# Single maxima between the groups of half sums and half differences in the front of a two-branch attention kernel

## The chip, the cores and the metric

The kernel runs on one core of one Trainium2 chip. The metric is the device time of one execution in microseconds (us). A measurement of a kernel is the median over several executions.

## The reference

For one sequence of 2048 positions and a model width of 512 the reference mixes two attention branches by a gate. Branch A is a local dilated attention (32 heads of 16, window of 8 keys with a stride of 2); branch B is a full attention whose 32 query heads share one key head and one value head.

```python
x = A_x
g = _sigmoid((x * gate_w).sum(-1, keepdims=True))
a = _A_ref(x, A_wqkv, A_wo)
b = _B_ref(x, B_wq, B_wk, B_wv, B_wo)
return g * a + (1 - g) * b
...
# branch B
q = (x @ wq).reshape(B, S, H, Dh).transpose(0, 2, 1, 3)
k = x @ wk
v = x @ wv
scores = jnp.einsum("bhqd,bkd->bhqk", q, k) * (Dh ** -0.5)
p = _softmax(scores, axis=-1)
o = jnp.einsum("bhqk,bkd->bhqd", p, v)
return o.transpose(0, 2, 1, 3).reshape(B, S, H * Dh) @ wo
```

The softmax of branch B takes the maximum of 2048 scores for every query and head off before the exponential, and these maxima are what this case is about.

## The kernel before

**The work on branch B.** The 2048 x 32 queries are cut into 32 units of 512 positions and 4 heads (`NU`). Queries lie with head dimensions on the partitions, and two heads share the 128 rows: head parity `odd` uses rows 64 * odd and up, so two matmuls on different row halves run side by side. The loop `for s in range(NS + 1)` (L1131) has 16 steps for each unit, 512 in all. A step computes the scores of 128 keys for two pairs of heads (`exp_pair`, L475, matmuls L480, exponential on ScalarE L482), and adds the weighted values of the step before into `po` (`weighted`, L487, eight row-and-column tiles of L490). The weighted values of a unit need its maxima: they stand in two extra rows of the query tile (rows 62 and 63 of each half), put there by `shift_a` to `shift_d`.

**The maxima.** A maximum here is over 512 keys, for 128 queries of one head; there are 2048 of them (`NF`), 64 for each unit. A slot `(v, pr, t, kc)` names two of them, one for each row half. There are three ways to compute them:

- `fill_pair` (L345): two matmuls into the two banks of `m2` (called `pm` in the profile) and one VectorE reduction over both (L350).
- `fill_one` (L354): one matmul into one bank, `m1` (`ps`) or another, and one VectorE reduction (L361). The second single of a slot waits in the list `half`.
- half sums and half differences: max(a, b) = (a + b)/2 + |a - b|/2. With the half sum and half difference of two blocks of keys in place of the keys (`half_keys`, `half_parts`, kept in `kcd`), `fill_diff` (L417) puts the differences of two slots into `m2`, ScalarE takes their absolute values into `dd` (L425), and later `fill_sum` (L430) puts the sums of one row half into a one-bank tile and a single VectorE instruction (L435) adds, reduces over the keys, and so finishes two maxima. `pend` lists sums still to come. Row half 0 goes into `m1`, row half 1 into `po`. In the front `dd` is one buffer; in the output rows it is two.

**The order.** Everything is issued in an order written out when the program is built. A planner keeps a time for each engine (`clk`), the time each bank comes free (`free`) and the time the absolute values are ready (`ready_d`), with fixed durations (`T_R` 0.23, `T_LAT` 0.20, `T_RED1` 0.61, `T_TTR` 0.66 us and so on), and decides by them what is issued next. Each engine then takes its instructions in that order.

**The front.** `stream` (L720) runs the projections in the front, and later the output rows. The two row halves of a projection are two sequences; where a single or a sum is due, it takes the place of one half's matmul and the other half goes on. In the front `pooled` is True, and `po` can take singles too. The front first projects the queries (lumps `q`, with `queries_post`), then branch A's queries, keys and values (64 lumps `a`, with `a_post`: two copies on ScalarE, L251 and L252, and additions on GpSimd). From the lumps (0, 3) to (0, 6) of branch A on, `half_sel` and `half_keys` make the half keys. From then on `paired` holds whenever two neighbouring slots can be taken together, and only differences and sums are issued, until two lumps before the end. Units are stacked (`stack`) up to the eighth in the front, and `fillable` admits only stacked units.

**The loop.** Each step may do one pair in `m2` and one single in `m1`. The single is issued only while `singles(s)` holds: twice the steps up to unit 31 plus 20 for each output row to come is less than what is left (`to_go`). When eight and four output rows are due (`out_phase`, L759), the stream runs again with `pooled` False and does half sums beside them. The last four rows are spread over the steps after the maxima (`spread`, products L836). If a unit's maxima come late, `pause` fills them in at once.

Of the kernel before, what the change touches and what calls it, by code (L numbers as in the profile page):

```python
# [49 lines left out]
def gated_mix_kernel(ctx, tc, xt, wa, wk, wq, wo_a, wo_b, out):  # L50
# [28 lines left out]
    m1 = pp.tile([P, 512], F32, name="ps")  # L79
    po = pp.tile([P, 512], F32, name="po")  # L80
# [5 lines left out]
    clk = {"pe": 0.0, "act": 0.0, "dve": 0.0}  # L86

    def after(eng, ready, dur):
        clk[eng] = max(clk[eng], ready) + dur
        return clk[eng]  # L90
# [214 lines left out]
    slots = [(v, pr, t, kc) for kc in range(2) for v in range(2) for pr in range(2) for t in range(4)]  # L305
    slots += [(v, pr, t, kc) for v in range(2) for pr in range(2) for t in range(4) for kc in range(2, 4)]
    slots += [(v, pr, t, kc) for v in range(2, NU) for pr in range(2) for t in range(4) for kc in range(4)]
    half = []
    free = {"m2": 0.0, "m1": 0.0, "e0": 0.0, "e1": 0.0, "po": 0.0}
    tasks, shifted, pm = [], set(), []  # L310
    hooks, pool, done = [], 0.0, set()
# [1 line left out]
    def fillable():  # L313
        return bool(half) or bool(slots) and slots[0][0] < len(stacked) and stacked[slots[0][0]] <= clk["pe"]

    def unit_tile(v):
        for x in (v, v + 1):
            if x < NU and x not in left:
                mx[x] = wp.tile([P, 2, 2, 4, 4], F32, name="mx", bufs=3)
                if pe:  # L320
                    nc.gpsimd.memset(mx[x], -FMAX)
                    charge(250)
                else:
                    nc.scalar.activation(mx[x].rearrange("p b i t k -> p (b i t k)"), ident[:, 0:64], AF.Identity, scale=0.0, bias=mk[:, 6:7])
                left[x] = NF // NU
        return mx[v]

    def max_mm(dst, v, pr, t, kc, odd):
        b = 64 * odd
        nc.tensor.matmul(dst, qst[home(v)[0]][b:b + 62, pr, t * P:(t + 1) * P], kst[b:b + 62, kc * 512:(kc + 1) * 512], start=True, stop=True)  # L330

    def to_go():
        return 2 * len(slots) + len(half)

    def filled(v, n):
        left[v] -= n
        if not left[v]:
            ms = wp.tile([P, 2, 2, 8], F32, name="ms")
            m = mx.pop(v).rearrange("p b i t k -> p b (i t) k")
            nc.vector.tensor_reduce(ms, m.unsqueeze(2).to_broadcast([P, 2, 2, 8, 4]), AX.X, ALU.max)  # L340
            mt = wp.tile([P, 32], F32, name="mt")
            nc.vector.transpose(mt, ms.rearrange("p b x y -> p (b x y)"))
            tasks.append((after("dve", 0, 0.66) + (2.0 if kcd and not pe else 0.1), shift_a, (v, mt)))
# [7 lines left out]
        free[key] = after("dve", after("pe", 0, T_R) + T_LAT, T_RED2) + 0.08  # L351
        filled(v, 2)

    def fill_one(dst=m1, key="m1"):  # L354
        if not half:
            v, pr, t, kc = slots.pop(0)
            half.extend([(v, pr, t, kc, 0), (v, pr, t, kc, 1)])
        v, pr, t, kc, odd = half.pop(0)
        m = unit_tile(v)
        max_mm(dst, v, pr, t, kc, odd)  # L360
        nc.vector.tensor_reduce(m[:, odd, pr, t, kc:kc + 1], dst, AX.X, ALU.max)  # L361
        free[key] = after("dve", after("pe", 0, T_R) + T_LAT, T_RED1) + 0.08
        filled(v, 1)


    sel, kcd, dd, pend, ready_d, formed, ended, wants = [], [], [], [], [0.0, 0.0], set(), set(), []
# [43 lines left out]
    def paired():  # L410
        return len(slots) > 1 and slots[0][3] % 2 == 0 and slots[0][3] // 2 in formed and slots[1] == slots[0][:3] + (slots[0][3] + 1,) and fillable()

    def half_mm(dst, v, pr, t, kc, x, odd):
        b = 64 * odd
        nc.tensor.matmul(dst, qst[home(v)[0]][b:b + 62, pr, t * P:(t + 1) * P], kcd[0][b:b + 62, kc // 2, x, :], start=True, stop=True)  # L415

    def fill_diff():  # L417
# [9 lines left out]
        free["m2"] = ready_d[1]  # L427
        pend.extend([(v, pr, t, kc, 0), (v, pr, t, kc, 1)])

    def fill_sum():  # L430
        v, pr, t, kc, odd = pend.pop(0)
        m = unit_tile(v)
        dst, key = ((m1, "m1"), (po, "po"))[odd]
        half_mm(dst, v, pr, t, kc, 0, odd)
        nc.vector.tensor_tensor_reduce(dd[0][:, odd], dst, dd[0][:, odd], 1.0, -FMAX, ALU.add, ALU.max, m[:, odd, pr, t, kc:kc + 1])  # L435
        free[key] = after("dve", max(clk["pe"] + T_R + T_LAT, ready_d[odd]), T_TTR) + 0.08
        filled(v, 2)
# [35 lines left out]
    pe, pexp, exped = [], {}, {}  # L473
# [246 lines left out]
    def stream(seq, mm, done, pooled):  # L720

        at, told = [0, 0], 0
        ended.clear()
        while min(at) < len(seq):
            single, odd = None, -1
            if wants and all(free[k] <= clk["pe"] + 0.1 for k in (("m1", "po") if wants[0] else ("m2",))):
                half_keys(wants.pop(0))
            if pend:
                if free[("m1", "po")[pend[0][4]]] <= clk["pe"] + 0.1 and ready_d[pend[0][4]] <= clk["pe"] + 0.4:
                    single, odd = fill_sum, pend[0][4]  # L730
            elif paired() and not half or 1 in wants:
                pass
            elif fillable() and free["m1"] <= clk["pe"] + 0.1:
                single, odd = lambda: fill_one(m1, "m1"), half[0][4] if half else 0
            elif pooled and fillable() and free["po"] <= clk["pe"] + 0.1:
                single, odd = lambda: fill_one(po, "po"), half[0][4] if half else 0
            dur = 0.0
            for b in (0, 1) if odd != 1 else (1, 0):
                if b == odd:
                    now = clk["pe"]  # L740
                    single()
                    clk["pe"] = now
                elif at[b] < len(seq):
                    dur = mm(b, seq[at[b]])
                    at[b] += 1
            after("pe", 0, dur or T_R)
            if ended or 0 in wants:
                pass
            elif paired():
                if not half and not pend and max(free["m2"], clk["dve"] - 1.2) <= clk["pe"] + 0.1:  # L750
                    fill_diff()
            elif slots and fillable() and free["m2"] <= clk["pe"] + 0.1:
                clk["pe"] = max(clk["pe"], free["m2"])
                fill_pair(m2, "m2")
            while told < min(at):
                told += 1
                done(seq[told - 1])

    def out_phase(js, n, whole_unit):  # L759

        m = 3 * (C + n)
        items = {}

        def mm(b, at):
            x, j, i = at
            if j not in items:
                items[j] = out_items(j, n)
                clk["pe"] = max(clk["pe"], free[f"e{x % 2}"])
            st, mv = items[j][i]
            h = slice(64 * b, 64 * b + 64)  # L770
            nc.tensor.matmul(eb[x % 2][:, b, :], st()[h], mv[h], start=(i == 0), stop=(i == m - 1))  # L771
            return T_R

        def done(at):
            x, j, i = at
            if i % 4 == 3:
                run_tasks()
                run_pool()
            if x == len(js) - 1 and i == m - 5:
                ended.add(1)  # L780
            if x == 0 and i == 1:
                turn(j, 1)
            if x == 0 and i == 6:
                later.pop(j)()
            if i == 3 * n and j != js[-1]:
                prepare(js[x + 1], n)
            if i == m - 5 and j != js[-1]:
                turn(js[x + 1], 1 - x % 2)
            if i == m - 1:
                out_store(j, x % 2)  # L790
                if j != js[-1]:
                    later.pop(js[x + 1])()

        if whole_unit:
            formed.update((0, 1))
            free["po"] = max(free["po"], clk["dve"] + 0.1)
            dd[:] = [px.tile([P, 2, 512], F32, name="pexp", bufs=6) for _ in range(2)]
        stream([(x, j, i) for x, j in enumerate(js) for i in range(m)], mm, done, False)
        while pend:
            odd = pend[0][4]  # L800
            clk["pe"] = max(clk["pe"], free[("m1", "po")[odd]], ready_d[odd] - 0.3)
            fill_sum()
            clk["pe"] += T_R
        settle("sum", 0)
        formed.clear()
# [309 lines left out]

    front = [(eb[1], "e1"), (eb[0], "e0"), (m2, "m2")]
    stream([(x, i) for x in range(len(lumps)) for i in range(3 * C)], mm, done_mm, True)
    assert not pend
    formed.clear()
    for kind in ("add", "store"):  # L1120
        settle(kind, 0)
# [9 lines left out]
    for s in range(NS + 1):  # L1131
# [11 lines left out]
        v = min(x[0][0] for x in (half, slots, [(NU,)]) if x)  # L1143
# [105 lines left out]
```

## Time and profile before

| | |
|---|---|
| median of 3 runs | 1487.6 us (1487.28 to 1487.6) |
| span of the profiled execution | 1485.2 us (2.4 us under the median; the execution's own time is not listed apart) |
| busy: PE, DVE, ACT, POOL | 1472.3, 1195.4, 1276.8, 1029.6 us |
| chain that ended last | PE 91%, ACT 3%, POOL 2% |
| costliest on ACT | exponentials L482, 988.4 us |
| costliest on DVE | pairs L350 623.6 us, singles L361 308.8 us |

The span is the time from the first to the last instruction of one profiled execution. Busy times are of the engine's own instructions; PE counts a matmul to its modelled end, so that a busy PE is not PE at its peak. In rows by instruction the columns are the line, the engine, the operation, what is written and read, and how often; then busy time and mean duration in ns; then the idle time just before, and who ended it. In rows by time the columns are start, duration, engine, line, operation and count, with the idle time before in brackets. PEld is the loading of weights, which runs beside PE.

### The profile page before, as it was taken

How to read it: one execution, taken by the hardware profiler on the slowest of the kernel's cores; microseconds unless marked ns; L12 is line 12 of the kernel's file. 1: busy time of each engine (PE TensorE's matmuls, PEld its weight loads, DVE VectorE, ACT ScalarE, POOL GpSimd, SP SyncE). 2: the span in 40 equal slices, each digit the busy share in tenths (PEclk: the TensorE clock that was granted, in tenths of full speed). 3: DMA queues.
4: the chain of work that ended last, by engine and by line, in shares of the span. 5: the costliest groups of instructions: out<-in, count | busy, mean ns of one | idle time of the engine just before them, and what ended most of it. 6: DMA issues, size and time to landing. Idle time of an engine off the chain costs nothing.

```text
span 1485.2 us, 29515 instructions
## 1 busy us (share of the span) xinstructions
PE 1472.3 (99%) x10996; PEld 707.2 (48%) x10996; DVE 1195.4 (80%) x1824; ACT 1276.8 (86%) x1654; POOL 1029.6 (69%) x1824
## 2 busy tenths in 40 slices
PE   9999999999999999999999999999999999999998
PEld 5999989433333333333333476333333363333343
DVE  6976667788888888888888888888888888888822
ACT  4468988999999999999999988999999978999975
POOL 7876988787888988988888999788797130110121
PEclk9999999999999999999999999999999999999999
DMA  6754233021120111211211202021020010000011
GB/s 222 210 151 135 88 105 107 28 84 52 55 85 18 67 59 41 70 41 41 70 43 40 81 31 89 12 70 51 31 70 12 12 34 19 2 1 1 16 30 43
DMA packets 54136, 89.86 MB, mean 60 GB/s; under 512 B 18849, under 2 KB 35289, under 8 KB 49769
## 3 DMA queue, kind: packets, MB, share of 16 engines
q1 hardware_dynamic: 46856, 48.98, 11.0%
q0 software_dynamic: 6560, 37.95, 7.6%
q8 instruction: 86, 1.41, 0.4%
q10 hardware_dynamic: 576, 1.05, 0.2%
q14 instruction: 58, 0.47, 0.1%
HBM read 60.07 MB, written 27.35 MB: 59 GB/s over the span
## 4 chain that ended last, share of the span: by engine, by line
PE 91%; ACT 3%; POOL 2%; issue 1%; DVE 1%; DMA 0%; DVEq 0%; POOLq 0%; ACTq 0%
PE po L490 34%; PE pe L480 26%; PE pm L330 8%; PE pe L1082 7%; PE ps L330 5%; PE pe L771 4%; PE pm L415 2%; PE ps L415 1%; PE pm L836 1%; PE po L415 1%; ACT dd L425 1%; POOL qlo L222 1%; POOL qraw L215 1%; PE pe L185 1%; ACT qhi L221 0%
## 5 line engine op out<-in xcount | busy, mean ns | idle before, releaser
L482 ACT ACTIVATE pexp<-pe 128x1024 f32<-128x1024 f32 x1022 | 988.4, 1022 | 102.7 <-PE pe L480 99.1
L350 DVE TENSOR_REDUCE mx<-pm 128x2 f32<-128x1024 f32 x511 | 623.6, 1220 | 143.8 <-PE pm L330 140.5
L490 PE MATMUL po<-pexp,vst 128*32 128x512 f32 x4096 | 545.5, 605 | 0.0
L480 PE MATMUL pe<-qst,kst 64*128 64x512 f32 x1916 | 523.6, 454 | 1.6 <-ACT pexp L482 1.0
L480 PEld LDWEIGHTS pe<-qst,kst 64*128 64x128 f32 x1916 | 215.2, 184 | 417.3 <-ACT pexp L482 408.2
L361 DVE TENSOR_REDUCE mx<-ps 128x1 f32<-128x512 f32 x454 | 308.8, 680 | 3.6 <-PE ps L330 3.5
L330 PE MATMUL pm<-kst,qst 62*128 62x512 f32 x971 | 197.7, 399 | 0.7 <-ACT pexp L482 0.4
L550 POOL TENSOR_TENSOR pr<-aext 128x256 f32<-128x256 f32 x256 | 182.1, 738 | 1.5 <-DMA aext<-ad 1.2
L330 PE MATMUL ps<-kst,qst 62*128 62x512 f32 x428 | 179.9, 420 | 0.0
L610 POOL TENSOR_TENSOR oa<-oa,av 128x256 f32<-128x256 f32 x224 | 164.0, 732 | 15.2
L490 PEld LDWEIGHTS po<-pexp,vst 128*32 128x32 f32 x4096 | 80.6, 108 | 176.3 <-issue 167.4
L607 POOL TENSOR_TENSOR av<-aext,lg 128x256 f32<-128x256 f32 x224 | 139.3, 622 | 12.5
L330 PEld LDWEIGHTS ps<-kst,qst 62*128 62x128 f32 x428 | 78.6, 184 | 69.3 <-DVE mx L361 65.9
L1082 PE MATMUL pe<-wal,xh 64*128 64x384 f32 (+1 forms) x504 | 109.9, 337 | 0.0
L1082 PE MATMUL pe<-wah,xh 64*128 64x384 f32 (+1 forms) x504 | 109.4, 338 | 0.4 <-ACT gate L255 0.4
L1082 PE MATMUL pe<-wah,xl 64*128 64x384 f32 (+1 forms) x504 | 109.6, 337 | 0.0
L516 POOL TENSOR_TENSOR rl<-rl,gate_t 128x16 f32<-128x16 f32 x31 | 6.9, 221 | 143.9 <-DVE rl L510 143.9
L425 ACT ACTIVATE dd<-pm 128x512 f32<-128x512 f32 x164 | 90.9, 607 | 17.8 <-PE pm L415 11.9
L435 DVE CUSTOM_DVE_ANT_0 dd<-ps,dd 128x512 f32<-128x512 f32 x82 | 56.7, 692 | 54.6 <-PE ps L415 29.5
L330 PEld LDWEIGHTS pm<-kst,qst 62*128 62x128 f32 x971 | 93.8, 187 | 6.3 <-DVE mx L350 3.2
L556 POOL TENSOR_TENSOR tr<-pr 128x512 f32<-128x512 f32 x64 | 81.7, 1276 | 4.2
L556 POOL TENSOR_TENSOR tr<-tr 128x256 f32<-128x256 f32 (+1 forms) x128 | 72.5, 566 | 7.9
(218 smaller groups left out, 1898.2 us busy)
## 6 DMA issues: line engine op xcount, KB each, us to landing
aext<-ad POOLq DMA_DIRECT2D x32, 1056.0 KB, 5.4
ad<-stage SPq DMA_DIRECT2D x32, 384.0 KB
qst<-qd SPq DMA_DIRECT2D x60, 128.0 KB
xraw<-xt SPq DMA_DIRECT2D x16, 256.0 KB
qd<-qhi SPq DMA_DIRECT2D x16, 256.0 KB
qd<-qlo SPq DMA_DIRECT2D x16, 256.0 KB
qst<-qd SPq DMA_DIRECT2D x60, 64.0 KB
qst<-ml SPq DMA_DIRECT2D x212, 2.0 KB
```

The source lines that it names most:

```text
L330: nc.tensor.matmul(dst, qst[home(v)[0]][b:b + 62, pr, t * P:(t + 1) * P], kst[b:b + 62, kc * 512:(kc + 1) * 512], start=True, stop=True)
L350: nc.vector.tensor_reduce(m[:, :, pr, t, kc], dst, AX.X, ALU.max)
L361: nc.vector.tensor_reduce(m[:, odd, pr, t, kc:kc + 1], dst, AX.X, ALU.max)
L425: nc.scalar.activation(dd[0][:, odd], m2[:, odd, :], AF.Abs)
L480: nc.tensor.matmul(bank[:, odd, :], kst[b:b + 64, kt * P:(kt + 1) * P], qst[home(u)[0]][b:b + 64, pr, :], start=True, stop=True)
L482: nc.scalar.activation(e, bank, AF.Exp, scale=SCALE)
L490: nc.tensor.matmul(po[32 * i:32 * i + 32, :], vst[:, kt, :], pexp[s, i // 2][:, i % 2, :], start=(kt == 0), stop=(kt == NJ - 1))
L550: nc.gpsimd.tensor_mul(pr[:, k], q, e[:, o:o + NH, AC:2 * AC])
L556: nc.gpsimd.tensor_add(nx, cur[:, :, 0:n], cur[:, :, n:2 * n])
L607: nc.gpsimd.tensor_mul(av, e[:, o:o + NH, 2 * AC:].rearrange("p j (h d) -> p j h d", d=DH), lg[:, w].unsqueeze(3).to_broadcast([P, NH, AG, ...
L610: nc.gpsimd.tensor_add(ao, ao, av)
L1082: nc.tensor.matmul(front[2 if x == last else x % 2][0][:, b, :n], l[h], r[h], start=(i == 0), stop=(i == 3 * C - 1))
```

## The change

In the front, once half keys exist, a list `extra` is kept beside `half`. When no sum is pending, or the next pending sum is at least 0.6 us from ready by plan, when VectorE's planned end is at most 0.45 us ahead of PE, and when `m1` or `po` is free, a single maximum is issued from `extra` into whichever of the two comes free first. If `extra` is empty, two neighbouring slots are taken off and become four singles. `fill_sum` also takes whichever of `m1` and `po` comes free first (`bank_free`), no longer one by row half. What is left in `extra` when the front ends goes to the head of `half`. `to_go` counts `extra` too.

```diff
--- before.py
+++ after.py
@@ -305,7 +305,7 @@
     slots = [(v, pr, t, kc) for kc in range(2) for v in range(2) for pr in range(2) for t in range(4)]
     slots += [(v, pr, t, kc) for v in range(2) for pr in range(2) for t in range(4) for kc in range(2, 4)]
     slots += [(v, pr, t, kc) for v in range(2, NU) for pr in range(2) for t in range(4) for kc in range(4)]
-    half = []
+    half, extra = [], []
     free = {"m2": 0.0, "m1": 0.0, "e0": 0.0, "e1": 0.0, "po": 0.0}
     tasks, shifted, pm = [], set(), []
     hooks, pool, done = [], 0.0, set()
@@ -330,7 +330,7 @@
         nc.tensor.matmul(dst, qst[home(v)[0]][b:b + 62, pr, t * P:(t + 1) * P], kst[b:b + 62, kc * 512:(kc + 1) * 512], start=True, stop=True)
 
     def to_go():
-        return 2 * len(slots) + len(half)
+        return 2 * len(slots) + len(half) + len(extra)
 
     def filled(v, n):
         left[v] -= n
@@ -351,11 +351,11 @@
         free[key] = after("dve", after("pe", 0, T_R) + T_LAT, T_RED2) + 0.08
         filled(v, 2)
 
-    def fill_one(dst=m1, key="m1"):
-        if not half:
+    def fill_one(dst=m1, key="m1", queue=None):
+        if not half and not queue:
             v, pr, t, kc = slots.pop(0)
             half.extend([(v, pr, t, kc, 0), (v, pr, t, kc, 1)])
-        v, pr, t, kc, odd = half.pop(0)
+        v, pr, t, kc, odd = (queue or half).pop(0)
         m = unit_tile(v)
         max_mm(dst, v, pr, t, kc, odd)
         nc.vector.tensor_reduce(m[:, odd, pr, t, kc:kc + 1], dst, AX.X, ALU.max)
@@ -427,10 +427,13 @@
         free["m2"] = ready_d[1]
         pend.extend([(v, pr, t, kc, 0), (v, pr, t, kc, 1)])
 
+    def bank_free():
+        return min(((m1, "m1"), (po, "po")), key=lambda x: free[x[1]])
+
     def fill_sum():
         v, pr, t, kc, odd = pend.pop(0)
         m = unit_tile(v)
-        dst, key = ((m1, "m1"), (po, "po"))[odd]
+        dst, key = bank_free()
         half_mm(dst, v, pr, t, kc, 0, odd)
         nc.vector.tensor_tensor_reduce(dd[0][:, odd], dst, dd[0][:, odd], 1.0, -FMAX, ALU.add, ALU.max, m[:, odd, pr, t, kc:kc + 1])
         free[key] = after("dve", max(clk["pe"] + T_R + T_LAT, ready_d[odd]), T_TTR) + 0.08
@@ -725,9 +728,15 @@
             single, odd = None, -1
             if wants and all(free[k] <= clk["pe"] + 0.1 for k in (("m1", "po") if wants[0] else ("m2",))):
                 half_keys(wants.pop(0))
-            if pend:
-                if free[("m1", "po")[pend[0][4]]] <= clk["pe"] + 0.1 and ready_d[pend[0][4]] <= clk["pe"] + 0.4:
-                    single, odd = fill_sum, pend[0][4]
+            bank, key = bank_free()
+            if pend and free[key] <= clk["pe"] + 0.1 and ready_d[pend[0][4]] <= clk["pe"] + 0.4:
+                single, odd = fill_sum, pend[0][4]
+            elif pooled and (extra or paired()) and not half and not wants and free[key] <= clk["pe"] + 0.1 and clk["dve"] <= clk["pe"] + 0.45 and (not pend or ready_d[pend[0][4]] >= clk["pe"] + 0.6):
+                if not extra:
+                    extra.extend(x + (odd,) for x in (slots.pop(0), slots.pop(0)) for odd in range(2))
+                single, odd = lambda: fill_one(bank, key, extra), extra[0][4]
+            elif pend:
+                pass
             elif paired() and not half or 1 in wants:
                 pass
             elif fillable() and free["m1"] <= clk["pe"] + 0.1:
@@ -798,7 +807,7 @@
         stream([(x, j, i) for x, j in enumerate(js) for i in range(m)], mm, done, False)
         while pend:
             odd = pend[0][4]
-            clk["pe"] = max(clk["pe"], free[("m1", "po")[odd]], ready_d[odd] - 0.3)
+            clk["pe"] = max(clk["pe"], free[bank_free()[1]], ready_d[odd] - 0.3)
             fill_sum()
             clk["pe"] += T_R
         settle("sum", 0)
@@ -1116,6 +1125,7 @@
     front = [(eb[1], "e1"), (eb[0], "e0"), (m2, "m2")]
     stream([(x, i) for x in range(len(lumps)) for i in range(3 * C)], mm, done_mm, True)
     assert not pend
+    half[:0] = extra
     formed.clear()
     for kind in ("add", "store"):
         settle(kind, 0)
```

## The prediction

> **What bounds the kernel now.** I read the head of the page first, then the busy time of each engine by stage, then the instructions in order of time in one stretch of each stage, and last the waits of the front.
>
> ```profile
> span 1485.2 us, 29515 instructions
> PE 1472.3 (99%) x10996; PEld 707.2 (48%) x10996; DVE 1195.4 (80%) x1824; ACT 1276.8 (86%) x1654; POOL 1029.6 (69%) x1824
> ...
> 105.00:262.00 157.00, 155.99 (x1576) 142.82 (x1575) 106.76 (x330) 135.76 (x317) 129.71 (x204) 1.00 0.35 109
> ...
> 272.00:848.00 576.00, 575.23 (x4016) 205.59 (x4012) 499.16 (x607) 529.12 (x570) 492.35 (x940) 1.00 0.17 55
> ...
> 1227.00:1410.00 183.00, 183.00 (x1275) 64.30 (x1274) 157.97 (x189) 165.67 (x172) 19.92 (x46) 1.00 0.03 8
> ```
>
> The columns of the last three are PE, PEld, DVE, ACT, POOL, clock. 105 to 262 us is the part of the front in which half sums and half differences run beside the projections of branch A; 272 to 848 and 1227 to 1410 us are the loop over steps. PE is fed in all of them and the clock is full (1.00), so the time is the sum of what PE is given, plus short waits. DVE, which the change loads, has 157.00 - 106.76 = 50.2 us free in the front; ACT has 21.2. What a maximum costs on PE in the loop is read from five steps in a row (the eight weighted products start a step):
>
> ```profile
> 400.11 1.06 PE L490 MATMUL po<-pexp,vst 128*32 128x512 f32 x8
> ...
> 401.67 0.46 PE L330 MATMUL ps<-kst,qst 62*128 62x512 f32 x1
> ...
> 402.29 1.06 PE L490 MATMUL po<-pexp,vst 128*32 128x512 f32 x8
> ...
> 403.63 0.40 PE L330 MATMUL pm<-kst,qst 62*128 62x512 f32 x2
> ...
> 403.86 0.40 PE L480 MATMUL pe<-qst,kst 64*128 64x512 f32 x2
> ...
> 403.92 3.81 ACT L482 ACTIVATE pexp<-pe 128x1024 f32<-128x1024 f32 x4 [0.27 <-PE pe L480]
> ...
> 404.20 1.06 PE L490 MATMUL po<-pexp,vst 128*32 128x512 f32 x8
> ...
> 405.76 0.39 PE L330 MATMUL ps<-kst,qst 62*128 62x512 f32 x1
> ...
> 406.35 1.06 PE L490 MATMUL po<-pexp,vst 128*32 128x512 f32 x8
> ...
> 408.24 1.06 PE L490 MATMUL po<-pexp,vst 128*32 128x512 f32 x8
> ```
>
> Steps with a single maximum (`ps`) last 402.29 - 400.11 = 2.18 and 406.35 - 404.20 = 2.15 us, those without 404.20 - 402.29 = 1.91 and 408.24 - 406.35 = 1.89. A single costs about 0.26 us here; that fits one slot of a row-tiled pair (403.86 - 403.63 = 0.23), because its own row half has four matmuls between two weighted groups where the other has three. I take 0.25. No more can be had by it: four exponentials take 3.81 us, so 1.905 for the two of a step, and a step without a single is already as long as its exponentials.
>
> **What moves.** Nothing is added to the work as a whole: a single given out in the front is one less in the loop, where a single is only issued while more is left than the pairs of the remaining steps and the output rows can take. What is left after the front now is large enough that it is issued nearly to the end:
>
> ```profile
> L361 DVE TENSOR_REDUCE mx<-ps 128x1 f32<-128x512 f32 x454 | 308.8, 680 | 3.6 <-PE ps L330 3.5
> ...
> 0.00:267.00 267.00, 32.27 (x50) 1.00 0.47 143
> ...
> 0.00:267.00 267.00, 32.92 (x27) 1.00 0.47 143
> ...
> 0.00:267.00 267.00, 90.92 (x164) 1.00 0.47 143
> ```
>
> The last three are the front's instructions of L361 (50 singles), of L350 (27 pairs) and of L425 (164 absolute differences, each of which with its sum stands for two maxima): 50 + 54 + 328 = 432 of 2048. Eight units of queries are stacked in the front, 8 x 64 = 512 maxima, so at most 80 more can be done there at all.
>
> **How many singles.** Each needs DVE for 0.68 us (L361's mean); 50.2 us of idle DVE hold at most 50.2 / 0.68 = 74. The condition asks for more than idle time: a bank free, DVE's planned end within 0.45 us, and the next sum at least 0.6 us off (or none pending). The waits of 105 to 262 us say how often that can be:
>
> ```profile
> DVE dd L435 <- PE ps L415: 29.3, 51, 1.2
> DVE dd L435 <- ACT dd L425: 17.1, 22, 1.2
> ACT dd L425 <- PE pm L415: 11.3, 18, 0.9
> PEld pm L415 <- ACT dd L425: 10.6, 37, 0.6
> ...
> ACT dd L425 <- DVE mx L435: 4.5, 8, 0.9
> ...
> L251 ACT ACTIVATE stage<-pe 128x384 f32<-128x384 f32 x53 | 26.1, 492 | 3.9 <-PE pe L1082 2.3 <-POOL wal L84 0.8 <-issue 0.2
> ```
>
> DVE waits 73 times for a sum, (29.3 + 17.1) / 73 = 0.64 us on average and up to 1.2. With the planner's constants, a difference that finds ACT free has its first absolute value ready 0.23 + 0.20 + 0.52 + 0.10 = 1.05 us after its issue, while the sums before it keep DVE booked to 0.9 or 1.0 after it: once the booking is within 0.45, the next sum is no more than 0.6 off, and no single fits. Where a projection block's two copies stand ahead on ACT (0.8 us in the plan), the sum is up to 0.8 later and one fits. There are 53 such blocks in the stretch. Between the half of 73 waits that are above their mean (37) and one for each block (53) I take 45 singles.
>
> **What they cost in the front.** Projection pairs follow each other here:
>
> ```profile
> 160.26 0.35 PE L1082 MATMUL pe<-wah,xl 64*128 64x384 f32 x2
> ...
> 160.43 0.35 PE L1082 MATMUL pe<-wah,xh 64*128 64x384 f32 x2
> ...
> 160.61 0.35 PE L1082 MATMUL pe<-wal,xh 64*128 64x384 f32 x2
> ```
>
> 0.175 us for a pair. 53 blocks x 12 pairs x 0.175 = 111 us; 156 / 2 = 78 differences in the stretch (a count of L425's instructions there, 78/79 by L435) at 0.23 for the pair of differences and 2 x 0.115 for the two sums, 36 us. 111 + 36 = 147, and 10.6 us of PE's weight loads waiting for ACT makes 158 of 157. So the account closes, and a single in the front costs half a slot, 0.23 / 2 = 0.115 us: the stream lets it take one row half while the other goes on with the projection, and evens the halves out. Gain for each: 0.25 - 0.115 = 0.135 us.
>
> To this comes a wait w for each single, which the trace of before does not show. Below: a longer cycle between two differences can swallow part of the 10.6 us that PE waits for ACT, 10.6 / 45 = 0.24 each at the very most. Above: PE runs in order, and if a single pushes the following sum by its whole DVE time, 0.68, and this comes back to PE through ACT, it is 0.68. The condition keeps the single out of the way of the next sum by plan (0.45 + 0.61 of DVE against 0.6 + 0.4 + latency of the sum's matmul), so I take the value near the rows that exist: ACT has waited for DVE's sums 8 times, 4.5 us in all, and if half of the singles bring one such short push of about 0.15, w is near 0.05 net. 45 x (0.135 - 0.05) = 3.8 us.
>
> That sums take whichever bank is free costs nothing by itself: without singles the two banks come free in turn as now. It is what lets a sum start while a single holds the other bank; without it, each single would hold up the sum of one parity. The same choice is made in the output rows' stream, where no singles are given out, and in turn again.
>
> **The end.** Now the maxima come too late for the last unit, and a pause is made for them:
>
> ```profile
> 1411.30 1.07 PE L490 MATMUL po<-pexp,vst 128*32 128x512 f32 x8
> ...
> 1413.43 1.06 PE L490 MATMUL po<-pexp,vst 128*32 128x512 f32 x8
> ...
> 1414.42 0.50 PE L330 MATMUL pe<-kst,qst 62*128 62x512 f32 x1
> ...
> 1416.31 3.83 ACT L482 ACTIVATE pexp<-pe 128x1024 f32<-128x1024 f32 x4 [1.48 <-PE pe L480]
> ...
> 1420.41 1.07 PE L490 MATMUL po<-pexp,vst 128*32 128x512 f32 x8
> ```
>
> Three steps last 1420.41 - 1411.30 = 9.1 us. Three bare steps, each a step without a single less its pair, 1.90 - 0.23 = 1.67, three pairs, one single and four row products (0.23 each) make 5.0 + 0.7 + 0.2 + 0.9 = 6.8. With 45 singles fewer to do, the pause has no cause; I count 1.8 of the 2.3 us, since the row products that would start earlier have to find something else to wait for.
>
> Sum: 3.8 + 1.8 = 5.6 us off the span of 1485.2, so 1479.6. The median of the runs stands 1487.6 - 1485.2 = 2.4 above that span, and the forecast is 1487.6 - 5.6 = 1482.0.
>
> **The rivals.** *Evacuation becomes the bound of the front (slower).* With 45 singles DVE carries 106.8 + 45 x 0.68 = 137 of 157 us, ACT 136. `dd` is one buffer: the next absolute value on ACT writes where DVE's sum still reads, ACT runs in order, and the difference after that finds m2 occupied, with every projection behind it on PE. For: 37 waits of PE's loads for ACT stand there already. Against: ACT has waited for DVE only 8 times. It decides from w = 0.135. At w = 0.30 the sum is 45 x (0.135 - 0.30) + 1.8 = -5.6, so 1493.2. The Trainium skill ("TensorEngine Tiling (Array Packing)", PSUM Bottleneck) states this rule: tiling speeds up TensorE but not the emptying of PSUM, which may become the bottleneck. By it the front, which runs row-tiled, is the wrong place for more reductions; the trace agrees only so far that PE waits 10.6 us of 157 for ACT, and DVE is at 68%.
>
> *The condition is rarely met.* If only 10 singles fit, 10 x 0.085 = 0.9 us and perhaps the pause's 1.0: 1485.7, no change that can be told. For: the waits of DVE average 0.64, hardly above 0.6.
>
> *More fit than I think.* 70 singles, which DVE's idle time and the 80 places still allow: 70 x 0.135 + 2.3 = 11.8, so 1475.8. For: each block of slow cycle grows longer with a single in it and makes room.
>
> **How the numbers follow.** A measurement of this kernel can tell about 0.2% from no change, 3 us. Forecast 0.52, evacuation 0.23, rarely met 0.14, more 0.11. Within the forecast, 37 to 53 singles and w from -0.03 to 0.12 give 37 x 0.015 + 1.0 = 1.6 to 53 x 0.165 + 2.3 = 11.0 us, 1476.6 to 1486.0; about one in eight of its cases is within 3 us. Faster: 0.11 + 0.46 = 0.57. Same: 0.14 + 0.06 = 0.20. Slower: 0.23. The range is 1476 to 1492: it leaves out the upper half of the evacuation rival (0.12) and a part of the last (0.05).
>
> **What would show it.** In the profile after: L361 out of `ps` and `po` by some 45 more before the first exponential, and as many fewer in the loop; the first exponential about 45 x (0.115 + 0.05) = 7 us later than now; the steps of 2.15 us stopping some twenty steps before the last unit; no wait of 1.48 us ahead of an exponential at the end. If the front ends over 11 us later, w is over 0.135 and the prediction is wrong by the evacuation; if it ends at the same time with under 20 more singles, by the condition. In the waits of the front, PE's loads for `pm` behind ACT should stay under 15 us.

## The result and the profile after

| | median | against the kernel before |
|---|---|---|
| before | 1487.37 us | |
| after | 1493.04 us (5 runs, 1492.86 to 1493.14) | 1.0037, 95% interval [1.0025, 1.0049] |

The change makes the kernel 5.7 us slower. The forecast was 1482.0, 5.6 us to the other side, and the measured time lies 1 us outside the range. The head of the page:

```profile
span 1491.2 us, 29554 instructions
PE 1477.2 (99%) x10996; PEld 710.0 (48%) x10996; DVE 1196.5 (80%) x1851; ACT 1281.4 (86%) x1664; POOL 1027.2 (69%) x1818
```

The busy time of PE, PEld, DVE, ACT and POOL by stage, with the clock, for the same three stages as before:

```profile
105.00:262.00 157.00, 156.91 (x1527) 138.30 (x1525) 136.44 (x369) 130.62 (x305) 124.33 (x201) 1.00 0.33 104
272.00:848.00 576.00, 573.12 (x4001) 207.57 (x3999) 470.49 (x586) 530.86 (x578) 483.15 (x923) 1.00 0.16 52
1227.00:1410.00 183.00, 182.78 (x1283) 67.88 (x1279) 156.73 (x199) 163.94 (x177) 17.69 (x42) 1.00 0.04 9
```

The same view up to 279 us, first of the front's singles alone (L361), then of the absolute differences alone (L425):

```profile
0.00:279.00 279.00, 71.08 (x107) 1.00 0.45 137
0.00:279.00 279.00, 94.75 (x170) 1.00 0.45 137
```

107 singles, the last of which is already the loop's, against 50: 56 more. 170 absolute values (two for each difference) against 164: three more differences, 12 more maxima. So 68 maxima moved. DVE fills the front as it should, 136.4 of 157 us against 106.8.

What it did to the time is read from the weighted products, a group of eight for each step. The first group of before, and then the trace of after in order of time, with start and duration in front:

```profile
269.41 1.07 PE L490 MATMUL po<-pexp,vst 128*32 128x512 f32 x8
...
281.50 1.07 PE L493 MATMUL po<-pexp,vst 128*32 128x512 f32 x8
...
291.88 3.85 ACT L485 ACTIVATE pexp<-pe 128x1024 f32<-128x1024 f32 x4 [0.17 <-PE pe L483]
...
295.90 3.85 ACT L485 ACTIVATE pexp<-pe 128x1024 f32<-128x1024 f32 x4 [0.17 <-PE pe L483]
...
301.94 16.00 ACT L485 ACTIVATE pexp<-pe 128x1024 f32<-128x1024 f32 x16
...
302.34 1.07 PE L493 MATMUL po<-pexp,vst 128*32 128x512 f32 x8
...
303.33 1.10 PE L483 MATMUL pe<-qst,kst 64*128 64x512 f32 x4
...
304.36 1.06 PE L493 MATMUL po<-pexp,vst 128*32 128x512 f32 x8
...
305.92 0.19 PEld L483 LDWEIGHTS pe<-qst,kst 64*128 64x128 f32 x2 [0.38 <-ACT pexp L485]
...
306.34 1.06 PE L493 MATMUL po<-pexp,vst 128*32 128x512 f32 x8
...
308.37 1.06 PE L493 MATMUL po<-pexp,vst 128*32 128x512 f32 x8
```

The front costs 281.50 - 269.41 = 12.1 us. And then 15 steps of the loop, groups 3 to 17, have no maximum at all: the 68 of the front have used up what could be computed of the eight stacked units, and the ninth is loaded only after step 16. Yet these steps are hardly shorter: 1.98 and 2.03 us. Sixteen exponentials, eight steps, take 16.00 us, and four with the gap before the next four take 295.90 - 291.88 = 4.02, so one step takes 2.0 us. Steps with a pair and a single last 2.15.

ScalarE alone doesn't set these 2.0 us. It waits 0.17 us for PE's scores before every four exponentials, and the row of sixteen holds gaps of up to 0.09 us that the merged row doesn't show. Where its scores are ready, four exponentials take 3.77 us and start 0.90 apart (at 495.54 in the trace of e11 below), 1.8 us for a step. PE waits for ScalarE as well (305.92, 0.38 us). By the starts of the single instructions, two steps are a round through both engines: weighted products at 302.34, scores at 303.33, two exponentials from 303.93 to 305.87, the next scores at 305.92, weighted products at 306.34, 4.00 us in all. That this round is the limit is read from the order of the instructions; no run changed it by itself.

The start of the same group in other kernels, less its start before (269.41, 312.22, 1398.80 and 1473.70 us), in us, group 0 being the first:

| run | singles in the front | group 0 | 20 | 480 | 511 |
|---|---|---|---|---|---|
| the change | 56 | 12.1 | 10.5 | 9.3 | 5.6 |
| e1_banks_only | 0 | 0.0 | 0.0 | 0.0 | 0.0 |
| e2_cap12 | 12 | 2.6 | 2.6 | 1.4 | -0.2 |
| e3_cap24 | 24 | 4.2 | 4.2 | 2.4 | -1.4 |
| e8_cap36 | 36 | 6.6 | 10.1 | 9.7 | 5.7 |
| e4_fixed_banks | 41 | 15.2 | 15.2 | 13.8 | 10.1 |
| e5_before_two_units | 0 | 0.0 | 10.9 | 11.3 | 11.3 |
| e6_after_two_units | 56 | 12.2 | 21.2 | 14.8 | 11.1 |
| e7_after_two_units_tight | 10 | 2.5 | 12.0 | 12.7 | 10.3 |
| e10_after_two_units_later | 56 | 12.1 | 12.3 | 7.5 | 3.8 |
| e9_before_two_units_later | 0 | 0.5 | 0.5 | 0.8 | 9.6 |
| e11_run_without_singles | 0 | 0.1 | 0.1 | 9.6 | 20.1 |

In the change the loop gives back 1.5 us in the empty steps, 1.2 up to group 480, and 3.7 in the last thirty groups. The sum of 12.1 - 1.5 - 1.2 - 3.7 is the 5.7 us of the result.

Where the maxima are computed, counted from the traces, says what the moved ones were taken from (the front here up to the first weighted products, so that 504 holds four singles of the loop's first step beside the 68; e3 is the change with 24 singles, e10 the change with two units more in reach, both described below):

| run | front | to group 18 | 18 to 480 | from 480 on |
|---|---|---|---|---|
| before | 432 | 52 | 1538 | 26 |
| e3_cap24 | 460 | 52 | 1530 | 6 |
| the change | 504 | 8 | 1530 | 6 |
| e10_after_two_units_later | 504 | 44 | 1500 | 0 |

From 24 to 56 singles, every further maximum comes out of the steps up to group 18 and none out of the rest of the loop. The front takes 7.9 us more for these 44, and the emptied steps return 1.6.

### The profile page after: what moved, and what is told of

It reads as the page before. It is cut to its first block, busy times and chain, and to the rows that moved or that the text cites. A ratio compares the mean times of both kernels' runs of the same rounds, so it can differ in the third digit from the quotient of the medians.

```text
span 1491.2 us, 29554 instructions
## 1 busy us (share of the span) xinstructions
PE 1477.2 (99%) x10996; PEld 710.0 (48%) x10996; DVE 1196.5 (80%) x1851; ACT 1281.4 (86%) x1664; POOL 1027.2 (69%) x1818
## 3 DMA queue, kind: packets, MB, share of 16 engines
q1 hardware_dynamic: 46928, 48.99, 11.1%
## 4 chain that ended last, share of the span: by engine, by line
PE 90%; ACT 4%; POOL 2%; DVE 1%; issue 1%; DVEq 0%; ACTq 0%; POOLq 0%
PE po L493 33%; PE pe L483 25%; PE pe L1091 8%; PE pm L330 7%; PE ps L330 5%; PE pe L780 4%; PE pm L415 3%; ACT pexp L485 2%; PE po L415 1%; PE ps L415 1%; PE pm L845 1%; POOL qlo L222 1%; POOL qraw L215 1%; PE pe L185 1%; ACT dd L425 1%
## 5 line engine op out<-in xcount | busy, mean ns | idle before, releaser
L350 DVE TENSOR_REDUCE mx<-pm 128x2 f32<-128x1024 f32 x484 | 590.8, 1221 | 145.2 <-PE pm L330 141.1
L483 PE MATMUL pe<-qst,kst 64*128 64x512 f32 x1916 | 518.4, 457 | 2.9 <-ACT pexp L485 2.0
L361 DVE TENSOR_REDUCE mx<-ps 128x1 f32<-128x512 f32 x459 | 312.2, 680 | 4.6 <-PE ps L330 4.0
L330 PE MATMUL ps<-kst,qst 62*128 62x512 f32 x449 | 188.6, 420 | 0.2 <-DVE mx L438 0.2
L610 POOL TENSOR_TENSOR av<-aext,lg 128x256 f32<-128x256 f32 x224 | 139.3, 622 | 12.7
L1091 PE MATMUL pe<-wah,xh 64*128 64x384 f32 (+1 forms) x504 | 128.2, 342 | 0.4 <-ACT gate L255 0.4
L1091 PE MATMUL pe<-wal,xh 64*128 64x384 f32 (+1 forms) x504 | 128.5, 341 | 0.0
L1091 PE MATMUL pe<-wah,xl 64*128 64x384 f32 (+1 forms) x504 | 126.9, 339 | 0.0
L425 ACT ACTIVATE dd<-pm 128x512 f32<-128x512 f32 x170 | 94.8, 608 | 24.9 <-PE pm L415 24.5
L330 PEld LDWEIGHTS ps<-kst,qst 62*128 62x128 f32 x449 | 82.6, 184 | 69.5 <-DVE mx L361 65.1
L1091 PEld LDWEIGHTS pe<-wah,xh 64*128 64x128 f32 x504 | 78.3, 186 | 2.5 <-ACT gate L255 0.8
L1091 PEld LDWEIGHTS pe<-wah,xl 64*128 64x128 f32 x504 | 78.7, 186 | 0.5
```

Source lines behind the costliest of these rows:

```text
L350: nc.vector.tensor_reduce(m[:, :, pr, t, kc], dst, AX.X, ALU.max)
L425: nc.scalar.activation(dd[0][:, odd], m2[:, odd, :], AF.Abs)
L483: nc.tensor.matmul(bank[:, odd, :], kst[b:b + 64, kt * P:(kt + 1) * P], qst[home(u)[0]][b:b + 64, pr, :], start=True, stop=True)
L610: nc.gpsimd.tensor_mul(av, e[:, o:o + NH, 2 * AC:].rearrange("p j (h d) -> p j h d", d=DH), lg[:, w].unsqueeze(3).to_broadcast([P, NH, AG, ...
L1091: nc.tensor.matmul(front[2 if x == last else x % 2][0][:, b, :n], l[h], r[h], start=(i == 0), stop=(i == 3 * C - 1))
```

## The experiments

Theory A: the loop's first steps run dry, and what was taken from them comes back nowhere. Theory B: a single costs the front more than the loop gives for it, and that is all.

**The banks alone.** The change without its singles (`taken` counts the pairs of slots that were given out as singles):

```diff
-            elif pooled and (extra or paired()) and not half and not wants and free[key] <= clk["pe"] + 0.1 and clk["dve"] <= clk["pe"] + 0.45 and (not pend or ready_d[pend[0][4]] >= clk["pe"] + 0.6):
+            elif pooled and (extra or len(taken) < 0 and paired()) and not half and not wants and free[key] <= clk["pe"] + 0.1 and clk["dve"] <= clk["pe"] + 0.45 and (not pend or ready_d[pend[0][4]] >= clk["pe"] + 0.6):
                 if not extra:
+                    taken.append(1)
```

> The change without its singles: only the free choice of the bank for the sums is left. Theory A (the loop's first steps run dry: 56 singles more in the front use up the units that are stacked, so that the steps 3 to 17 of the loop have no maximum to compute) and rival B (each single costs the front more than it saves the loop) both expect no difference from the kernel before, within 1 us, and the first exponential within 0.5 us of 266.6. A rival C, that the choice of the bank itself disturbs the front, expects some us of the 12 us there.

Measured: 1487.22 us, 0.9999 [0.9990, 1.0007]. The free choice of the bank does nothing alone. What moved is the singles' doing.

**Fewer singles.** The same edit with 3, 6 and 9 pairs of slots:

```diff
-            elif pooled and (extra or len(taken) < 0 and paired()) and not half
+            elif pooled and (extra or len(taken) < 6 and paired()) and not half
```

> The change with at most 12 singles given out in the front (3 pairs of slots). Theory A: the front is longer by 12 x 0.2 = 2.4 us, the loop's first steps keep their work (51 maxima of the 80 - 12 = 68 that are left to stacked units), and all 12 are taken from the end of the loop at 0.21 to 0.25 each, so -2.5 to -3.0 there: -0.5 us in all, between -1.5 and +0.5. Theory B: a share of the 5.7 us, 12 / 56 x 5.7 = +1.2 us.

> The change with at most 24 singles in the front (6 pairs of slots). Theory A: still under the knee, which lies near 512 - 432 - 52 = 28; the front is longer by 24 x 0.2 = 4.8 us, the steps 3 to 17 of the loop have their maxima and last 2.15 us, and the end of the loop gains 24 x 0.21 to 0.25 = 5.0 to 6.0: -0.7 us in all, between -2 and +1. Theory B: 24 / 56 x 5.7 = +2.4 us.

> The change with at most 36 singles in the front (9 pairs of slots), no units added. Theory A: beyond the knee at 24 to 28, so the singles above it bring back next to nothing: first exponential near 273.5, some 3 or 4 steps of the loop without a maximum just ahead of step 18, and 1486.0 + 10 x 0.18 = 1487.8 us, between 1487 and 1489. Without a knee, the line through 12 and 24 singles (1487.5 and 1486.0) would go on to 1484.5.

Measured: 1487.54 with 12 singles, 1.0001 [0.9992, 1.0010]; 1485.96 with 24, 0.9991 [0.9982, 1.0000]; 1493.01 with 36, 1.0039 [1.0027, 1.0052]. The first 24 bring a gain, 1.5 us at the edge of its interval, and theory B, which expected 2.4 us more with 24, is out in this form. The front pays 4.2 us for 24 singles and one more difference, 28 maxima, 0.15 each; the loop gives 5.6 us back. The knee is there, but 36 miss theory A's 1487 to 1489. Six steps (12 to 17) are empty, and then there is a wait that none of the theories had; the trace of e8 in order of time:

```profile
308.09 5.19 SPq L471 DMA_DIRECT2D q<-ml  x8
...
313.38 0.62 SPq L299 DMA_DIRECT2D qst<-qd  x1
...
316.72 0.50 PE L330 MATMUL pm<-kst,qst 62*128 62x512 f32 x1 [1.36 <-DMA qst<-qd]
...
318.09 0.76 PE L330 MATMUL pm<-kst,qst 62*128 62x512 f32 x1 [0.87 <-DMA qst<-qd]
...
319.35 1.02 ACT L485 ACTIVATE pexp<-pe 128x1024 f32<-128x1024 f32 x1 [2.87 <-PE pe L483]
```

The load of the ninth unit stands on the SP queue behind eight transfers of maxima and comes later than the 5 us of the plan; PE, in order, waits for it with the first maximum of that unit, and ScalarE stands 2.87 us. Groups 18 to 20 lose 4.2 us by it. Without that the run would stand at 1493.0 - 4.2 = 1488.8 by estimate, where theory A had it.

**The sums tied to their banks again, singles as they are:**

```diff
-        dst, key = bank_free()
+        dst, key = ((m1, "m1"), (po, "po"))[odd]
```

The two places that ask whether a sum's bank is free ask for that bank again.

> The change with the sums tied to their banks again (row half 0 into m1, row half 1 into po), singles as in the change. The singles are given out by the same conditions, so some 45 to 56 of them. If the free choice matters, sums now wait for the bank that a single holds, by plan and on PE, and the front is longer for each single than 12.1 / 56 = 0.22 us: first exponential at 279 us or later and 1493 to 1498 us in all. If it doesn't, the time is that of the change within 1 us.

Measured: 1497.94 us, 1.0071 [1.0058, 1.0083]; 41 singles for 15.2 us of front, 0.37 each (0.22 in the change), and one difference less. The waits of PE's weight loads in the front, this run first, then the change (columns: total, times, longest):

```profile
PEld pm L415 <- ACT dd L425: 12.6, 37, 0.4
PEld ps L415 <- DVE mx L361: 8.1, 37, 0.2
```

```profile
PEld pm L415 <- ACT dd L425: 8.7, 30, 0.4
PEld ps L415 <- DVE mx L361: 3.2, 16, 0.2
```

So the free choice is worthless alone, and necessary with the singles: without it, a sum that finds a single in its bank has to wait for it.

**Two units more for the loop's first steps.** If dry steps are the cause, the change should be saved by giving those steps something to do. `ob` has a second buffer that is idle until step 160; units 8 and 9 go there.

```diff
+    two_more = pe[0].tile([P, C, 512], F32R, name="ob", tag="ob", bufs=2)
+    for x in range(2):
+        qst.append(two_more[:, 2 * x:2 * x + 2])
+        clear(NB + x, nc.vector)
+        stack(NB + x)
```

`home` gives units 8 and 9 these tiles, and unit 10 the one of unit 0 and so on, so that later units come as early as before or earlier.

> The kernel before, with two units of queries more in reach of the loop's first steps: the tile ob has a second buffer that is idle until step 160, and units 8 and 9 are loaded there as the loop begins. The kernel before has 80 maxima left in stacked units at that point and uses 51 to 58 of them before the next unit comes in at step 17, so neither theory A nor theory B expects a gain: within 1 us of the kernel before, and no change in the maxima of the first 20 steps (58 matmuls).

> The changed kernel with the same two units more in reach of the loop's first steps, and the same 56 singles in the front. Theory A (the first steps run dry): steps 3 to 17 get their maxima back and last 2.15 us, 44 maxima fewer are left for later, and the singles end some 40 steps sooner at 0.25 us each: 1493.0 + 1.6 - 11 = 1483.6 us, between 1481.5 and 1486; the first exponential stays at 278.6. Theory B (the front's price is what makes the change slow): no change, 1493 within 1 us, or somewhat slower by the loads.

> As before, with stricter conditions for a single in the front: the planned end of VectorE at most 0.25 us ahead (0.45) and the next sum at least 0.8 us off (0.6). If part of the front's 0.22 us a single is waits that a late single causes (beyond the half slot of 0.115), there are fewer singles, some 35, each at 0.15 to 0.18 us, and the first exponential is at 272 to 273; the loop gives 0.25 for each. Then 1487.4 - 45 x 0.25 + 6 = 1482 to 1485 us. If the price is the same for all, 0.18 for each maximum, the time goes with the number alone: 35 / 56 of the gain of the run with the wide conditions.

Measured: 1497.74, 1499.06 and 1498.17 us (1.0070 [1.0057, 1.0082], 1.0077 [1.0064, 1.0090], 1.0073 [1.0059, 1.0087]): all three expectations missed, for a wait that the added lines bring. The trace of e5 in order of time:

```profile
273.77 0.91 DVE L163 MEMSET ob<- 32x1024 f32 x1 [7.03 <-DMA ad<-stage]
...
278.99 0.79 PE L330 MATMUL ps<-kst,q 62*128 62x512 f32 x1 [7.88 <-DVE mx L361]
```

The memory of `ob` is that of the front's staging tiles, whose last store is still on its way; VectorE waits 7.03 us for it, and PE behind VectorE. It happens once, so the rest of the traces can be read. In e6 the empty steps are gone, and from group 3 (21.6 us late) to 511 (11.1) the loop gives back 10.5 us, where the change gives 6.5. But 41 fewer matmuls of maxima between groups 400 and 480 gave only 21.2 - 14.8 less 2.0 before group 400, 4.4 us: 0.11 each and not 0.25. The trace of e6 there, in steps with a pair and no single:

```profile
1382.90 3.84 ACT L485 ACTIVATE pexp<-pe 128x1024 f32<-128x1024 f32 x4 [0.19 <-PE pe L483]
1383.20 1.06 PE L493 MATMUL po<-pexp,vst 128*32 128x512 f32 x8
1385.33 1.07 PE L493 MATMUL po<-pexp,vst 128*32 128x512 f32 x8
1386.93 3.84 ACT L485 ACTIVATE pexp<-pe 128x1024 f32<-128x1024 f32 x4 [0.19 <-PE pe L483]
1387.23 1.06 PE L493 MATMUL po<-pexp,vst 128*32 128x512 f32 x8
1389.35 1.07 PE L493 MATMUL po<-pexp,vst 128*32 128x512 f32 x8
```

The steps alternate, 2.13, 1.90, 2.12 us, and average 2.01, the same as the empty steps above. Of two steps without a single only one is short. With that theory A fell in its numbers, and A2 took its place: in a run of such steps a single is worth what a step stands above 2.01 us, 0.15 at most.

e7 asked whether stricter conditions make singles cheaper in the front:

```diff
-clk["dve"] <= clk["pe"] + 0.45 and (not pend or ready_d[pend[0][4]] >= clk["pe"] + 0.6)
+clk["dve"] <= clk["pe"] + 0.25 and (not pend or ready_d[pend[0][4]] >= clk["pe"] + 0.8)
```

It left 10 singles and one more difference, 14 maxima for 2.5 us: 0.18 each, as dear as the 68 of the change. The price isn't that of a few late singles.

**The same, without the wait.** GpSimd clears the tiles at steps 2 and 3, and the loads are issued at steps 4 and 6:

```diff
+        if s in (2, 3):
+            clear(NB + s - 2, nc.gpsimd)
+            charge(2000)
+        if s in (4, 6):
+            stack(NB + (s - 4) // 2)
```

> The kernel before with units 8 and 9 in the idle second buffer of ob, as in the earlier run, but cleared by GpSimd at steps 2 and 3 and loaded at steps 4 and 6. In the earlier run VectorE cleared them as the loop began and waited 7.0 us for the last store out of the front's tiles, whose place they take, and the loop lost 10.8 us there, once. Without that wait: within 1.5 us of the kernel before, 58 matmuls of maxima in the first 20 steps.

> The changed kernel with the same. Theory A as it was (44 maxima lost to empty steps, each single in the loop worth 0.25 us): some 6 empty steps are left, 26 maxima more come back in the first 18 steps, and 1493.0 - 26 x 0.25 = 1486.5 us. Theory A2, after the earlier run's trace (in a run of steps without singles a step is 2.01 us, set by ScalarE, so that a single is worth only 0.15 there, and the gain at the end is had with 24 singles already): 1493.0 - 26 x 0.15 + 1 = 1489 to 1490 us, still slower than before. Theory B (only the front counts): 1493.

Measured: the change with the two units 1491.20, 1.0025 [1.0015, 1.0036]; the kernel before with them 1496.70, 1.0064 [1.0051, 1.0077]. With only two empty steps left the change gains 1.8 us (5.6 to 3.8 at group 511) and is still slower than before. Theory A (1486.5) is wrong in size, A2 (1489 to 1490) nearer and 1 to 2 us too low. By this run, running dry costs 1.8 of the 5.7 us; it may be somewhat more, since two steps are still empty and the kernel before with the same lines stands 0.8 later at group 480. The kernel before missed its expectation by 8 us, and where it lost them tells what the end is worth. Its trace at groups 480 to 488:

```profile
1419.09 0.50 PE L330 MATMUL pe<-kst,qst 62*128 62x512 f32 x2 [0.64 <-DVE mx L350]
...
1421.35 0.50 PE L330 MATMUL pm<-kst,qst 62*128 62x512 f32 x2 [0.62 <-DVE mx L350]
...
1424.50 1.94 ACT L482 ACTIVATE pexp<-pe 128x1024 f32<-128x1024 f32 x2 [8.58 <-PE pe L480]
```

Here 268 and not 272 absolute values were made in all, 8 maxima less, and from group 480 on 40 maxima are left and not 26. They are made up in a pause in which ScalarE waits 8.58 us. From group 480 to 511 the run loses 9.6 - 0.8 = 8.8 us, 0.6 for each of the 14. Why fewer differences fitted in is not shown.

**A single priced by itself.** The kernel before with no singles in steps 100 to 139:

```diff
-                if not later_rows and (kt or not s or u >= NU - 8) and singles(s):
+                if not 100 <= s < 140 and not later_rows and (kt or not s or u >= NU - 8) and singles(s):
```

> The kernel before, with no single issued in steps 100 to 139 of the loop, to price a single by itself: the 40 steps hold pairs only (some 4 of them had no single anyway). If a single costs 0.25 us as in the prediction, step 140 comes 36 x 0.25 = 9 us sooner than in the kernel before. If a run of such steps is set by ScalarE at 2.01 us, 36 x 0.15 = 5.4 us sooner. At the end the 36 come late, and the whole is slower than before, by how much neither says.

Measured: 1507.30 us in one run, slower as expected, since the singles come late at the end. The singles of steps 100 to 139 lie between groups 98 and 138. Group 98 stands where it did before and group 138 3.6 sooner: 3.6 us for 35 singles, 0.10 each, less than either figure. Its trace at groups 104 to 107:

```profile
491.08 1.06 PE L490 MATMUL po<-pexp,vst 128*32 128x512 f32 x8
492.98 1.06 PE L490 MATMUL po<-pexp,vst 128*32 128x512 f32 x8
...
494.50 1.15 ACT L83 ACTIVATE woh<-os 128x512 fp32r<-128x512 f32 x2
...
495.10 1.06 PE L490 MATMUL po<-pexp,vst 128*32 128x512 f32 x8
...
495.54 3.77 ACT L482 ACTIVATE pexp<-pe 128x1024 f32<-128x1024 f32 x4
...
497.96 0.64 PE L490 MATMUL po<-pexp,vst 128*32 128x512 f32 x4
```

1.90 and 2.12 again; and the step in which ScalarE has two copies of an output weight to make (1.15 us) lasts 2.86, where the same step of the kernel before, with its single, lasts 2.59, so that less is saved there.

The traces of the two kernels together show the rule behind all these prices. Two neighbouring steps with a pair each, outside the output rows, last 4.31 us with a single in both (331 times in the kernel before), 4.04 with a single in one of them (105 times) and 4.02 with none (39 times in e11; all medians). The first single taken out of two steps saves 0.27 us, the second 0.02. Of the 20 pairs of steps in e11 15 had both singles before, which makes 15 x 0.29 + 5 x 0.02 = 4.5 us; of the 0.9 that are missing from it, 0.27 are at the copies shown.

## Why the prediction was wrong

**The step that failed: a single is worth 0.25 us in the loop.** I read it from steps with and without a single next to each other, 2.15 and 1.90, and took 1.905 for what two exponentials need. For one step between steps with singles the figure is right (4.31 - 4.04 = 0.27). But the moved maxima are missing in runs of neighbouring steps, and there the second of two saves 0.02. Over such a run the price is 0.10 (e11) to 0.11 (e6), and the front asks 0.15 (e3) to 0.18 (the change) for a maximum. With 0.25 - 0.115 the change was a gain for any number of singles; with these prices it is none for any number, and the only gain is the end's. The premise that failed with it is that the time is the sum of what PE is given: from 286.0 to 316.4 us PE is busy for 29.04 of 30.40 us, in steps with hardly a maximum, and the busy share doesn't tell that these steps wait on a round through PE and ScalarE. I also named ScalarE the limit of such steps; it isn't full in them.

**The number.** Forecast 45 singles, at most 53 within the forecast; it was 56, and with the longer blocks three more differences: 68 maxima. The limit of 80 that I had worked out was used for a bound only. That the loop up to group 18 lives on the same 80 places, with 52 maxima of its own, I missed, and so the rival that the loop runs dry. All 44 maxima beyond those of e3 came out of these steps, at 1.6 us for 44, 0.04 each. By e10, refilling most of the steps wins 1.8 of the 5.7 us back. The rest is what theory B names: the front asks more for a maximum than the loop gives.

**The front's price held.** 12.1 us over 68 maxima is 0.18, against 0.115 + 0.05 forecast. PE's slots explain 68 x 0.115 = 7.8, and its weight loads wait 2.7 us more than before for ScalarE and VectorE together (8.7 + 3.2 + 1.2 + 0.6 against 11.0, and some smaller ones on both sides); about 1.6 us of the 12.1 I can't place. First weighted products 12.1 and not 7 us later: nearly all by the number.

**The end held, and was worth more.** Forecast 1.8 us, measured 3.7 (9.3 to 5.6 in the change, 2.4 to -1.4 with 24 singles, 1.4 to -0.2 with 12); this holds the pause and 20 maxima less from group 480 on. With 24 singles all of it is earned. That is why 24 win 1.5 us (4.2 in the front against 1.8 in the loop and 3.8 at the end) and 56 lose 5.7.

**The rival of evacuation gave 1493.2, and the time was 1493.0, by chance.** Its mechanism was a wait of 0.30 us for each single; the wait beyond the slots is (12.1 - 7.8) / 56 = 0.08, under the 0.135 at which it decides. The sign that I had set for it, a front over 11 us longer, did come, but it was worked out for 45 singles and says nothing with 68 maxima. VectorE is at 87% of the stretch, and PE's loads wait 13.7 us for it and ScalarE, 2.7 more than before. The rule that I put beside it (the Trainium skill, "TensorEngine Tiling (Array Packing)", PSUM Bottleneck; the page names it for a fourfold speedup, and the front's pairs are twofold) is not what this case turned on. Nearest to it comes e4, where a bank is held: PE's loads wait 21.0 us, and the front pays 0.37 us for a single.

The version with 24 singles is the best that was run: 1485.96 us, 0.9991 [0.9982, 1.0000] of the kernel before, and faster than the change.

## What to carry to other kernels

Price a removed instruction from a run of steps without it, and from two neighbouring steps together, not from a lone one: here the first of two was worth 0.27 us and the second 0.02. By these figures a loop that leaves out the single of every second step would keep most of the 0.27 each time, more than the front asks; that is an estimate, and no run tried it. When work is moved ahead, ask what the place it came from does instead, and whether the work that is ready there was counted. And find out which of the moved pieces were late: here the first 28 maxima earned all that the end had to give, 3.8 us, and the 44 after them nothing there.

## What the runs showed of the hardware

Exponentials over 128x1024 elements whose scores were ready started 0.90 us apart, though each is shown 1.02 to 1.06 long (four in 3.77 us in e11). A merged row without a gap can still hold waits: sixteen took 16.00 us in the change, with gaps of up to 0.09 us between them. A clearing of a tile on VectorE waited 7.03 us for a store out of other tiles whose memory it reused (e5), and the loop lost 10.8 us by it, once.
